# Attention and a two-matrix feed-forward on one core: the mean of the layer norm taken from the state's product by sums of float16 halves, paired high halves for the state's reads, and a new order of the work

## The chip, the cores and the metric

The kernel runs on one core of one Trainium2 chip. The metric is device time in microseconds (us) of one execution; lower is better. The kernel before took 707.6 us, the median of three runs (705.15 to 709.07).

The core has engines with queues of their own, each worked off in order: TensorE (PE in the profile, with its weight loads as PEld), VectorE (DVE), ScalarE (ACT), GpSimd (POOL), and SyncE (SP), which here only issues transfers. They meet through semaphores.

## What is computed

Cut to what matters, with B = 8 batches, H = 8 heads, S = 512 rows, Ns = 32 state rows per head and D = 64; the feed-forward's weights are 512x2048 and 2048x512:

```python
scores = scale * x @ state.T            # per batch and head, 512 x 32
xread  = softmax(scores) @ state        # 512 x 64 per head
scores2 = scale * state @ x.T           # 32 x 512
sread  = softmax(scores2) @ x           # 32 x 64 per head
x = concatenate([xread, sread])         # heads side by side: 544 rows of 512 per batch
mu, var = mean(x), mean((x - mu) ** 2)  # over the 512 columns
xn = (x - mu) / sqrt(var + 1e-06) * g_ln
out = x + maximum(xn @ w_ch1, 0) @ w_ch2
```

x and state come as float32, the weights as float64. Every large product is made of float16 halves: a high half and what is left of the number after it. A product of two such numbers is three matmuls (high by high, high by low, low by high), and with the halves laid side by side on the partitions sometimes fewer.

## The kernel before

**Row form.** The 512 rows of one batch never exist as normalized rows. Since xread is the softmax `ea` times the state, `xread @ w1` is `ea` times (`state @ w1`). So for each batch a `matrix` is made of the state and the first weight (`state_products`, lines 577 to 591: eight matmuls of 32x512 on four column groups at once, line 582, into one PSUM tile `acc`, for each of four units u of 512 hidden columns and two groups g of four heads). ScalarE takes its high half out of PSUM (line 590), VectorE the low half (line 591). `first_products` (line 605) multiplies `matrix` by `ea` (matmuls of line 616) into `acc`; `hidden` (line 595) takes each tile through a buffer `strip`, of which there are three: ScalarE writes the relu into `strip`, ScalarE the high half `hid`, and an engine subtracts for the low half. `second_products` (line 677) multiplies `hid` by the second weight (line 673), and VectorE adds the result to the residual `xr`.

**The mean.** Subtracting the row's mean is done on the weight before: `weights1(u)` (lines 498 to 538) loads float64 words (`raw`), makes float32 of them (`words`, `w_t`), gets the mean over the 512 rows of gain times weight by four float32 matmuls (`means`, line 516), and replaces `w_t` by gain times weight less that mean (line 519: four VectorE instructions on 128x512). Then ScalarE takes sizes (line 521), bfloat16 matmuls add them up (line 525), a scale comes of the largest sum, and the weight is split in a high and a low half (line 531, 128x2048 at once). Four transfers (line 538) lay the halves out as `w1c`: for each k of 128 rows, index s of 0 or 1 picks 64 rows, which stand on the partitions twice, as high half and as low half.

**The state's own rows.** The 8x32 rows `sread` of all batches go to DRAM, come back as two tiles of 128 rows, and are normalized and split in `state_hidden` (line 636). Their product with `w1c` (line 657) is 16 matmuls of 128x256 for each 128 hidden columns: eight with the high half of the rows standing twice, eight with the low half standing twice. 4 units, 4 times 128 columns each, make 256 matmuls.

**Order of the work.** Every step is yielded by a generator as one item; `issue` (line 190) takes items of several generators by strings such as "c3 c1 a0-1", a letter for the generator and numbers for its items. `PLAN` orders the prologue (weights, batch 0 with products taken by units, batch 1, attention of batch 2), `BATCH` one round for each of the batches 2 to 5 (products of batch b with the attention and the state products of b + 1), `LAST` the rest. So the order on each engine's queue is what these strings say. Transfers are nearly all on SP's queue.

**Names used below.** `s_j` is the state of a batch, laid out 32 rows of four heads on the partitions; `x_am` the largest size in it, from which its scale comes; `sh` its halves; `sT` these, transposed by a transfer. `banks` is the one PSUM tile of two banks that attention uses in turn: for scores (line 320), for the read of x by the softmax (line 396) and its fold (line 409), out of which VectorE takes `sread`, and for `mix` (line 432), which multiplies `ek` (a copy of `ea`, made by eight transfers and one more) by `sk` (halves of `s_r`, the state again). `mix` takes the tile over from `sread`.

Of the kernel before, what the change touches and what calls it, by code (L numbers as in the profile page):

```python
# [113 lines left out]
def moe_attention(ctx: ExitStack, tc: tile.TileContext, x, state, g_ln, w1, w2, out):  # L114

# [656 lines left out]
```

## Time and profile before

| what | us |
|---|---|
| median of three runs | 707.6 |
| profiled execution, its own time | 707.91 |
| its span in the trace | 706.1 |
| PE busy in the span | 655.7 |
| DVE busy | 370.9 |
| ACT busy | 365.3 |
| POOL busy | 68.0 |

The span is what the trace covers; the profiled execution took 1.8 us more than it. In the profile a group of instructions is named by line, engine, operation and output<-input; a line can be that of a helper (line 110 is the one that runs most items), so groups are told apart by their tiles. "Idle before" is the time that the engine stood still just before such instructions, with what released it. Matmuls are pipelined, so the mean of one matmul's record is longer than the step from one to the next; the chain of waits shows the step.

### The profile page before, as it was taken

How to read it: one execution, taken by the hardware profiler on the slowest of the kernel's cores; microseconds unless marked ns; L12 is line 12 of the kernel's file. 1: busy time of each engine (PE TensorE's matmuls, PEld its weight loads, DVE VectorE, ACT ScalarE, POOL GpSimd, SP SyncE). 2: the span in 40 equal slices, each digit the busy share in tenths (PEclk: the TensorE clock that was granted, in tenths of full speed). 3: DMA queues.
4: the chain of work that ended last, by engine and by line, in shares of the span. 5: the costliest groups of instructions: out<-in, count | busy, mean ns of one | idle time of the engine just before them, and what ended most of it. 6: DMA issues, size and time to landing. Idle time of an engine off the chain costs nothing.

```text
span 706.1 us, 10278 instructions
## 1 busy us (share of the span) xinstructions
PE 655.7 (93%) x4129; PEld 320.8 (45%) x4132; DVE 370.9 (53%) x670; ACT 365.3 (52%) x588; POOL 68.0 (10%) x54
## 2 busy tenths in 40 slices
PE   1565989999999999899999999999999999999997
PEld 0232645444453444444444444444444345445763
DVE  5995889655624454354635462545365834421120
ACT  5585889986413933295419541773287545410220
POOL 0000463211200002000200020002000200000000
PEclk9867899999999999999999999999999999999999
DMA  8988794636251032503070306130524060140001
GB/s 325 326 217 197 232 209 119 123 74 135 59 138 61 8 60 55 148 30 68 16 185 32 68 8 162 63 64 8 124 90 68 1 135 5 59 61 1 31 31 30
DMA packets 97392, 67.52 MB, mean 96 GB/s; under 512 B 73600, under 2 KB 89472, under 8 KB 96896
## 3 DMA queue, kind: packets, MB, share of 16 engines
q1 hardware_dynamic: 95424, 63.19, 35.1%
q0 software_dynamic: 864, 3.15, 2.5%
q8 instruction: 32, 0.52, 0.3%
q10 hardware_dynamic: 1056, 0.53, 0.3%
q14 instruction: 16, 0.13, 0.1%
HBM read 28.05 MB, written 9.44 MB: 53 GB/s over the span
## 4 chain that ended last, share of the span: by engine, by line
PE 70%; DVE 9%; DMA 8%; SPq 5%; ACT 4%; POOL 2%; issue 1%; POOLq 0%; DVEq 0%; ACTq 0%
PE acc L673 37%; PE acc L616 20%; SPq L110 5%; PE acc L657 4%; PE acc L582 3%; DMA w1c<-raw 2%; POOL ts L110 2%; DVE w_t L110 2%; PE acc L516 2%; DMA s_j<-in_state_dram 1%; DMA s_r<-in_state_dram 1%; PE banks L432 1%; DMA raw<-in_moe_w_ch_dram 1%; DVE raw L110 1%; DMA ebT<-eb 1%
## 5 line engine op out<-in xcount | busy, mean ns | idle before, releaser
L673 PE MATMUL acc<-w2h,hid 128*128 128x512 f16 x1632 | 368.2, 382 | 0.0
L673 PEld LDWEIGHTS <-hid 128*128 128x128 f16 x1632 | 158.2, 99 | 192.7 <-issue 12.6
L616 PE MATMUL acc<-ea,matrix 128*128 128x512 f16 (+1 forms) x864 | 176.1, 356 | 1.0 <-DVE matrix L110 0.7
L616 PEld LDWEIGHTS <-matrix 128*128 128x128 f16 x864 | 82.6, 98 | 84.6 <-issue 5.5
L110 DVE TENSOR_TENSOR hid<-strip,hid 128x512 f16<-128x512 f32 x120 | 81.2, 697 | 71.4 <-ACT hid L110 71.1
L110 ACT ACTIVATE strip<-acc,hs 128x512 f32<-128x512 f32 x112 | 75.5, 681 | 53.5 <-PE acc L616 29.6
L110 ACT ACTIVATE hid<-strip 128x512 f16<-128x512 f32 x136 | 83.0, 626 | 7.6 <-PE acc L673 4.9
L110 ACT ACTIVATE matrix<-acc 128x512 f16<-128x512 f32 x64 | 36.2, 602 | 64.1 <-PE acc L582 64.1
L110 DVE SCALAR_TENSOR_TENSOR xr<-acc,of_second,xr 128x512 f32<-128x512 f32 x28 | 21.0, 748 | 64.7 <-PE acc L673 64.6
L110 DVE SCALAR_TENSOR_TENSOR matrix<-acc,matrix 128x512 f16<-128x512 f32 x64 | 41.8, 680 | 20.8 <-ACT matrix L110 20.7
L582 PE MATMUL acc<-w1c,sT 128*32 128x512 f16 x512 | 38.2, 397 | 10.7 <-DMA w1c<-raw 10.3
L110 POOL TENSOR_TENSOR ts<-ts,mA 128x1024 f32<-128x1024 f32 (+1 forms) x8 | 16.1, 2016 | 232.8 <-DVE mA L110 202.6
L110 ACT ACTIVATE strip<-acc,hr 128x512 f32<-128x512 f32 x8 | 5.4, 686 | 49.4 <-PE acc L657 49.4
L110 POOL TENSOR_TENSOR rs<-rs,mhalf 128x4 f32<-128x4 f32 (+1 forms) x10 | 9.5, 955 | 199.6 <-DVE rs L110 199.6
L657 PE MATMUL acc<-xsT,w1c 128*128 128x256 f16 x256 | 28.4, 273 | 0.0
L110 POOL TENSOR_TENSOR hid<-strip,hid 128x512 f16<-128x512 f32 x16 | 22.1, 1405 | 58.7 <-ACT hid L110 58.6
L110 DVE SCALAR_TENSOR_TENSOR x<-x_f,x_s,x 128x512 f16<-128x512 f32 x32 | 25.3, 804 | 4.4 <-ACT x L110 4.3
L657 PEld LDWEIGHTS <-w1c 128*128 128x128 f16 x256 | 25.1, 98 | 3.5
L110 ACT ACTIVATE xr<-banks,ux 128x1024 f32<-128x1024 f32 x14 | 15.7, 1119 | 20.2 <-PE banks L432 20.2
L110 ACT ACTIVATE ea<-ef 128x1024 f16<-128x1024 f32 (+1 forms) x9 | 8.5, 958 | 33.5 <-DVE ef L110 33.5
L110 DVE BATCH_NORM_STATS2 s<-xr 128x6 f32<-128x512 f32 x32 | 21.4, 686 | 8.1 <-ACT xr L110 7.5
L582 PEld LDWEIGHTS <-sT 128*32 128x32 f16 x512 | 10.4, 97 | 30.5 <-issue 24.0
(112 smaller groups left out, 514.4 us busy)
## 6 DMA issues: line engine op xcount, KB each, us to landing
raw<-in_moe_w_ch_dram SPq DMA_DIRECT2D x16, 1024.0 KB, 8.2
out_dram<-xr SPq DMA_DIRECT2D x16, 512.0 KB, 2.7
x_f<-in_x_dram SPq DMA_DIRECT2D x15, 512.0 KB, 5.9
w1c<-raw SPq DMA_DIRECT2D x16, 256.0 KB, 6.9
ek<-ea SPq DMA_DIRECT2D x56, 64.0 KB, 2.1
ek<-ek SPq DMA_DIRECT2D x7, 512.0 KB, 4.4
xr<-part POOLq DMA_DIRECT2D x6, 512.0 KB, 5.3
s_r<-in_state_dram SPq DMA_DIRECT2D x28, 64.0 KB, 4.1
```

The lines of the kernel that those rows point to most:

```text
L110: return lambda: f(*map(now, args), **{k: now(v) for k, v in kw.items()})
L432: nc.tensor.matmul(px[:, c, D * h:D * h + D], lhsT=ek[:, h // 4, h % 4, (2 * t + c) * P:(2 * t + c + 1) * P], rhs=sk[:, h], start=True, st ...
L516: nc.tensor.matmul(ps, lhsT=gm[:, k:k + 1].broadcast_to([P, P]), rhs=t4[:, k], start=k == 0, stop=k == 3)
L582: nc.tensor.matmul(ps[32 * j:32 * j + 32], lhsT=sT[:, g, a, 32 * j:32 * j + 32], rhs=w[:, 2 * g + j // 2, j % 2], start=a == 0, stop=a == ...
L616: nc.tensor.matmul(o, lhsT=m[:, g, i, P * q:P * q + P], rhs=ea[:, s, k, g], start=g == 0 and n == 0 and (b > 0 or q % 2 == 0), stop=g == 1 ...
L657: nc.tensor.matmul(ps[:, 256 * f:256 * f + 256].rearrange("p (t n) -> p t n", t=2), lhsT=w[:, k // 2, k % 2, P * (q + f):P * (q + f) + P], ...
L673: nc.tensor.matmul(po, lhsT=hid[:, i, q, c * P:(c + 1) * P], rhs=w[:, j, q], start=first and q == 0 and n == 0, stop=last and q == 3 and n ...
```

## The change

**The mean** is no longer taken from the weight. The gain goes into the split: a column `gs` is gain times scale, and the split is done for each k by itself, in quarters of 128x512. Sizes are taken of the weight without gain, and the adding matmuls have the gain (`gb`) as their other side. Eight float16 matmuls (`add_up`) sum the split halves over all rows, and ScalarE keeps the result, `sums_of_inputs[:, u]`, in the buffer `convert`, which is thereby no longer free for raw words. For each batch VectorE makes `mean`, the mean of each state row (two small instructions). In `state_products` VectorE now first writes a `strip`: sums times mean, plus the tile in PSUM (the mean has a minus sign); both halves of `matrix` are taken of the strip.

**The state's rows.** Before their product, eight transfers (`high_halves`) put the high halves of two neighbouring 64-row pieces on one set of 128 partitions, in the buffers `extra_0` and `extra_1`. The low half of the rows is transposed once, not twice, and multiplied by these: four matmuls in place of eight, 12 in place of 16.

**Order.** All three strings are new. Two of the four last stores of each tile of the state's rows go to ScalarE's queue. Constants CM and SB change by a factor of two.

The core of the diff:

```diff
 PLAN = (
-    "b1 b3-4 b2 b0 b5 a0 b6-11 b22 b72 b12 d0 d3 b23-25 b13 b15 b14 b17-18 d2 d4 d1 d6 b19-20 d5 d7 e1 e5-6 e0 "
+    "d0 b0-1 b3 b2 b4-6 b16 b7-12 b17 c1 c0 d1 a0 d3 b24-25 b21-22 b13-14 b26-27 c6 b15 e1 c5 c7 e0 b18 c3 m2 "
...
     def gain():
-        yield do(nc.vector.tensor_scalar, gm, gx, 1.0 / DM, None, ALU.mult)
+        yield do(nc.scalar.activation, gb, gx.unsqueeze(2).broadcast_to([P, C, P]), AF.Abs, scale=1.0 / SW)
...
+        mean = Later(lambda: main.tile([P, G], F32, name=f"mean_{b % 2}"))
+        yield do(nc.vector.tensor_reduce, mean, sj, AX.X, ALU.add)
+        yield do(nc.vector.tensor_scalar, mean, mean, sst, -1.0 / DM, ALU.mult, ALU.mult)
...
         raws = ((wide(0, "raw"), wide(1, "raw")), (wide(2, "raw"), wide(3, "raw")), (extra(0, "raw"), extra(1, "raw")),
-                (odd("raw"), spare("raw")))[u]
+                (odd("raw"), wide(0, "raw")))[u]
...
-        def means(ps, t4):
-            for k in range(4):
-                nc.tensor.matmul(ps, lhsT=gm[:, k:k + 1].broadcast_to([P, P]), rhs=t4[:, k], start=k == 0, stop=k == 3)
-        yield do(means, ps, t4)
-        for k in range(4):
-            yield do(nc.vector.scalar_tensor_tensor, t4[:, k], t4[:, k], gx[:, k:k + 1], ps, ALU.mult, ALU.subtract)
...
+        yield do(nc.vector.tensor_scalar, gs, gx, scale, None, ALU.mult)
         hl = raws[1].bitcast(F16).rearrange("p (i e) -> p i e", i=2)
-        yield from split(hl[:, 0], hl[:, 1], t, scale)
+        for k in range(4):
+            yield from split(*(hl[:, i, 512 * k:512 * k + 512] for i in range(2)), t4[:, k], gs[:, k:k + 1])
...
+        def add_up(ps, hl):
+            for i in range(2):
+                for k in range(4):
+                    nc.tensor.matmul(ps, lhsT=ones, rhs=hl[:, i, k], start=i == 0 and k == 0, stop=i == 1 and k == 3)
+        yield do(add_up, ps, hl)
+        yield do(nc.scalar.activation, sums_of_inputs[:, u], ps, AF.Copy)
...
                 yield do(multiply, ps, g, sT, w1c[u])
-                yield do(nc.scalar.activation, m[:, g, 0], ps, AF.Copy, scale=CM)
-                yield do(nc.vector.scalar_tensor_tensor, m[:, g, 1], ps, CM, m[:, g, 0], ALU.mult, ALU.subtract)
+                strips[0] += 1
+                v = block(2, f"strip_{strips[0] % 3}", 1, "strip")
+                yield do(nc.vector.scalar_tensor_tensor, v, sums_of_inputs[:, u], mean[:, g:g + 1], ps, ALU.mult, ALU.add)
+                yield do(nc.scalar.activation, m[:, g, 0], v, AF.Copy, scale=CM)
+                yield do(nc.vector.scalar_tensor_tensor, m[:, g, 1], v, CM, m[:, g, 0], ALU.mult, ALU.subtract)
...
+    def high_halves():
+
+        for t in range(2):
+            pair = extra(t, "high").bitcast(F16).rearrange("p (u k f) -> p u k f", u=2, k=4)
+            for u in (2 * t, 2 * t + 1):
+                high[u] = pair[:, u % 2]
+                for s in range(2):
+                    half = slice(64 * s, 64 * s + 64)
+                    yield do(nc.sync.dma_start, out=high[u][half], in_=w1c[u][half, :, s])
...
-                for k in range(H):
-                    for a in range(2):
-                        nc.tensor.matmul(ps[:, 256 * f:256 * f + 256].rearrange("p (t n) -> p t n", t=2),
-                                         lhsT=w[:, k // 2, k % 2, P * (q + f):P * (q + f) + P], rhs=xsT[:, :, a, k],
-                                         start=f == 0 and k == 0 and a == 0, stop=k == H - 1 and a == 1,
-                                         skip_group_check=True)
+                fs = slice(P * (q + f), P * (q + f) + P)
+                for k in range(12):
+                    nc.tensor.matmul(ps[:, 256 * f:256 * f + 256].rearrange("p (t n) -> p t n", t=2),
+                                     lhsT=w[:, k // 2, k % 2, fs] if k < H else wn[:, k - H, fs], rhs=xsT[:, :, k],
+                                     start=f == 0 and k == 0, stop=k == 11, skip_group_check=True)
...
-            yield do(nc.sync.dma_start, out=out[4 * t + j, S:S + NS, :], in_=results[B][0][1][t][32 * j:32 * j + 32, 0])
+            yield do((nc.sync, nc.scalar)[j % 2].dma_start, out=out[4 * t + j, S:S + NS, :],
+                     in_=results[B][0][1][t][32 * j:32 * j + 32, 0])
```

**What the strings move, at three places.** The number behind a tile's name only tells one use of it from another.

First, VectorE's queue in a round of `BATCH`, around `sread`. Before:

```order
L110 TENSOR_SCALAR rB_3393<-rB_3393,x_i_3083 128x2
L110 TENSOR_REDUCE x_am_3670<-s_j_3668 128x1
L110 TENSOR_TENSOR sread_3502<-banks_3421,rB_3393 128x128
L110 SCALAR_TENSOR_TENSOR matrix_3500<-acc_3491,matrix_3500 128x512
L110 SCALAR_TENSOR_TENSOR xr_2839<-acc_3156,of_second_3389,xr_2839 128x512
L110 BN_STATS s6_3531<-xr_3529 128x6
```

And now:

```order
L113 SCALAR_TENSOR_TENSOR strip_3627<-sums_370,mean_0_3125,acc_3606 128x512
L113 SCALAR_TENSOR_TENSOR strip_3629<-sums_370,mean_0_3125,acc_3618 128x512
L113 SCALAR_TENSOR_TENSOR xr_2982<-acc_3477,of_second_3247,xr_2982 128x512
L113 TENSOR_SCALAR rB_3490<-rB_3490,x_i_3213 128x2
L113 TENSOR_TENSOR sread_3651<-banks_3573,rB_3490 128x128
L113 SCALAR_TENSOR_TENSOR matrix_3555<-strip_3629,matrix_3555 128x512
L113 SCALAR_TENSOR_TENSOR matrix_3653<-strip_3627,matrix_3653 128x512
```

Ahead of `sread` stood `x_am`, which reads the next batch's `s_j`. It has moved behind, into the next round, and two strips stand a little ahead of `sread` instead.

Second, SP's queue in the same round, from the state's transpose to the next batch's loads. Before:

```order
L110 DMA_TRANSPOSE sT_0_3153<-sh_92 128x4x128
L110 DMA_TRANSPOSE xT_3241<-x16_2986 128x16x128 x2
L110 DMA s_r_3645<-in_state_dram 32x8x64
L110 DMA ek_3385<-ea_3381 32x2x512 x2
L110 DMA_TRANSPOSE ebT_3419<-eb_3369 128x16x128
L110 DMA ek_3385<-ea_3381 32x2x512 x6
L110 DMA ek_3385<-ek_3385 64x4096
L110 DMA x_f_3647<-in_x_dram 128x4x256
L110 DMA s_r_3645<-in_state_dram 32x8x64
L110 DMA s_j_3668<-in_state_dram 128x2x64
```

And now:

```order
L113 DMA_TRANSPOSE sT_0_3223<-sh_92 128x4x128
L113 DMA s_r_3070<-in_state_dram 32x8x64
L113 DMA s_j_3777<-in_state_dram 128x2x64
L113 DMA_TRANSPOSE xT_3376<-x16_3132 128x16x128
L113 DMA s_r_3070<-in_state_dram 32x8x64
L113 DMA_TRANSPOSE xT_3376<-x16_3132 128x16x128
L113 DMA_TRANSPOSE ebT_3474<-eb_3471 128x16x128
L113 DMA s_r_3779<-in_state_dram 32x8x64
L113 DMA ek_3497<-ea_3495 32x2x512 x8
L113 DMA ek_3497<-ek_3497 64x4096
```

The next batch's `s_j` has moved from behind the copies of `ek` to a place right behind `sT`, ahead of both transposes of x, and the transpose `ebT` no longer stands between the copies.

Third, VectorE's queue in the prologue, at the first split of a weight (unit 0). Before:

```order
L110 SCALAR_TENSOR_TENSOR w1_t_181<-w1_t_181,gx_75,acc_296 128x512 x2
L110 SCALAR_TENSOR_TENSOR ea_290<-ef_288,ea_290 128x512
L110 SCALAR_TENSOR_TENSOR w1_t_181<-w1_t_181,gx_75,acc_296 128x512
L110 RECIPROCAL of_weights_217<-is1_262 128x1
L110 SCALAR_TENSOR_TENSOR eb_307<-eB_304,eb_307 128x1024
L110 SCALAR_TENSOR_TENSOR raw_142<-w1_t_140,of_weights_217,raw_142 128x2048
```

And now:

```order
L113 TENSOR_SCALAR gs_0_217<-gx_75,of_weights_205 128x4
L113 SCALAR_TENSOR_TENSOR w1_t_203<-raw_152 128x1024
L113 TENSOR_SCALAR is1_212<-of_weights_205 128x1
L113 SCALAR_TENSOR_TENSOR raw_129<-w1_t_150,gs_0_217,raw_129 128x512
L113 STREAM_TRANSPOSE ts_233<-banks_194 128x512
L113 RECIPROCAL of_weights_205<-is1_212 128x1
```

The low half of unit 0 stood as one piece behind the gain's instructions of unit 2 and part of batch 0's softmax; now its first quarter stands two instructions behind its column `gs`.

More of the change, by code (lines that the diff above doesn't have):

```diff
@@ L28 @@
 SW = 2.0**13
-CM = 2.0**-14
+CM = 2.0**-15
 SH = 2.0**-12
-SB = 2.0**14
+SB = 2.0**15
 SR = 2.0**-6
@@ L223, in moe_attention @@
     nc.vector.memset(mhalf, -0.5)
-    ones = main.tile([P, P], BF16, name="ones")
-    nc.vector.memset(ones, 1.0 / SW)
+    ones = main.tile([P, P], F16, name="ones")
+    nc.vector.memset(ones, 1.0)
     ids = main.tile([P, 2, 2], F32, name="ids")
@@ L248, in absmax @@
         return do(nc.vector.tensor_reduce, a, t, AX.X, ALU.max, apply_absolute_value=True)
-    gm = main.tile([P, C], F32, name="gm")
+    gb = main.tile([P, C, P], BF16, name="gb")
+    sums_of_inputs = block(8, "convert", 1, "sums").rearrange("p (u f) -> p u f", u=U)
     def gain():
-        yield do(nc.vector.tensor_scalar, gm, gx, 1.0 / DM, None, ALU.mult)
+        yield do(nc.scalar.activation, gb, gx.unsqueeze(2).broadcast_to([P, C, P]), AF.Abs, scale=1.0 / SW)
     sh = main.tile([P, G, 2, 2, D], F16, name="sh")
@@ L329, in attention @@
         ea = block(4, f"ea_{b % 2}", 1, "ea").bitcast(F16).rearrange("p (s i g t) -> p s i g t", s=parts, i=2, g=G)
-        results.append((residual(b, "xr"), sT, ea, Later(lambda: main.tile([P, C], F32, name=f"rf_{b % 2}"))))
+        results.append((residual(b, "xr"), sT, ea, Later(lambda: main.tile([P, C], F32, name=f"rf_{b % 2}")), mean))
         mA, dA = column("mA", 32), column("dA", 32)
@@ L506, in weights1 @@
         raws = ((wide(0, "raw"), wide(1, "raw")), (wide(2, "raw"), wide(3, "raw")), (extra(0, "raw"), extra(1, "raw")),
-                (odd("raw"), spare("raw")))[u]
+                (odd("raw"), wide(0, "raw")))[u]
         t = unit(u, "w1_t")
         scale, m = of_weights[:, u, 0:1], of_weights[:, u, 2:3]
+        gs = Later(lambda: main.tile([P, C], F32, name=f"gs_{u}"))
         yield from words(src, raws, t)
         t4 = t.rearrange("p (k f) -> p k f", k=4)
-        ps, total = accumulator(), accumulator()
-        def means(ps, t4):
-            for k in range(4):
-                nc.tensor.matmul(ps, lhsT=gm[:, k:k + 1].broadcast_to([P, P]), rhs=t4[:, k], start=k == 0, stop=k == 3)
-        yield do(means, ps, t4)
-        for k in range(4):
-            yield do(nc.vector.scalar_tensor_tensor, t4[:, k], t4[:, k], gx[:, k:k + 1], ps, ALU.mult, ALU.subtract)
         sizes = raws[0].bitcast(BF16)[:, 0:2048]
         yield do(nc.scalar.activation, sizes, t, AF.Abs)
+        total, ps = accumulator(), accumulator()
         def add(total, v):
             for k in range(4):
-                nc.tensor.matmul(total, lhsT=ones, rhs=v[:, 512 * k:512 * k + 512], start=k == 0, stop=k == 3)
+                nc.tensor.matmul(total, lhsT=gb[:, k], rhs=v[:, 512 * k:512 * k + 512], start=k == 0, stop=k == 3)
         yield do(add, total, sizes)
@@ L546, in weights2 @@
         raws = ((wide(2, "raw"), wide(3, "raw")), (extra(0, "raw"), extra(1, "raw")), (odd("raw"), wide(3, "raw")),
-                (extra(1, "raw"), spare("raw")))[u]
-        t = (wide(1, "w2_t"), spare("w2_t"), extra(0, "w2_t"), odd("w2_t"))[u]
+                (extra(1, "raw"), wide(3, "raw")))[u]
+        t = (wide(1, "w2_t"), wide(2, "w2_t"), extra(0, "w2_t"), odd("w2_t"))[u]
         s, am, m, top, inv = (of_weights[:, U + u, k:k + 1] for k in range(5))
@@ L575, in moe_attention @@
     matrix = [[None] * U for _ in range(B)]
+    strips = [0]
     def state_products(b):
@@ L583, in multiply @@
                                      rhs=w[:, 2 * g + j // 2, j % 2], start=a == 0, stop=a == 1, skip_group_check=True)
-        sT = results[b][1]
+        sT, mean = results[b][1], results[b][4]
         for u in range(U):
@@ L589, in state_products @@
                 yield do(multiply, ps, g, sT, w1c[u])
-                yield do(nc.scalar.activation, m[:, g, 0], ps, AF.Copy, scale=CM)
-                yield do(nc.vector.scalar_tensor_tensor, m[:, g, 1], ps, CM, m[:, g, 0], ALU.mult, ALU.subtract)
-    strips = [0]
+                strips[0] += 1
[3 more added lines that the diff above has]
+                yield do(nc.vector.scalar_tensor_tensor, m[:, g, 1], v, CM, m[:, g, 0], ALU.mult, ALU.subtract)
     def hidden(ps, scale, hi, lo, n, engine=nc.vector):
@@ L634, in first_products @@
                                           nc.gpsimd)
+    high = [None] * U
+    def high_halves():
[6 more added lines that the diff above has]
+                    yield do(nc.sync.dma_start, out=high[u][half], in_=w1c[u][half, :, s])
     def state_hidden():
         xr = results[B][0][1]
-        xsT = rows("xsT").bitcast(F16).rearrange("p (t a h n) -> p t a h n", t=2, a=2, h=H)
+        xsT = rows("xsT").bitcast(F16)[:, 0:24 * P].rearrange("p (t k n) -> p t k n", t=2, k=12)
         mv, rs = yield from moments([xr[t][:, 0] for t in range(2)])
@@ L643, in state_hidden, with multiply @@
             yield do(nc.vector.tensor_scalar, xn, xr[t][:, 0], mv[:, t, 0:1], rs[:, t:t + 1], ALU.subtract, ALU.mult)
-            v = xn.rearrange("p (h d) -> p h d", h=H).unsqueeze(2).broadcast_to([P, H, 2, D])
-            pc = halves("pc").rearrange("p (a h i d) -> p a h i d", a=2, h=H, i=2)
-            yield do(nc.scalar.activation, pc[:, 0], v, AF.Copy, scale=SN)
-            for i in range(2):
-                yield do(nc.vector.scalar_tensor_tensor, pc[:, 1, :, i], xn.rearrange("p (h d) -> p h d", h=H), SN,
-                         pc[:, 0, :, i], ALU.mult, ALU.subtract)
-            yield do(nc.sync.dma_start_transpose, out=xsT[:, t].rearrange("p a h n -> p (a h) n"),
-                     in_=pc.rearrange("p a h i d -> p (a h i d)"))
-        def multiply(ps, q, w, xsT):
-            for f in range(2):
-                for k in range(H):
-                    for a in range(2):
-                        nc.tensor.matmul(ps[:, 256 * f:256 * f + 256].rearrange("p (t n) -> p t n", t=2),
-                                         lhsT=w[:, k // 2, k % 2, P * (q + f):P * (q + f) + P], rhs=xsT[:, :, a, k],
-                                         start=f == 0 and k == 0 and a == 0, stop=k == H - 1 and a == 1,
-                                         skip_group_check=True)
+            v = xn.rearrange("p (h d) -> p h d", h=H)
+            pc = halves("pc")[:, 0:12 * P]
+            hi = pc[:, 0:8 * P].rearrange("p (h i d) -> p h i d", h=H, i=2)
+            lo = pc[:, 8 * P:12 * P].rearrange("p (h d) -> p h d", h=H)
+            yield do(nc.scalar.activation, hi, v.unsqueeze(2).broadcast_to([P, H, 2, D]), AF.Copy, scale=SN)
+            yield do(nc.vector.scalar_tensor_tensor, lo, v, SN, hi[:, :, 0], ALU.mult, ALU.subtract)
+            yield do(nc.sync.dma_start_transpose, out=xsT[:, t], in_=pc)
+        def multiply(ps, q, w, wn, xsT):
+            for f in range(2):
+                fs = slice(P * (q + f), P * (q + f) + P)
[3 more added lines that the diff above has]
+                                     start=f == 0 and k == 0, stop=k == 11, skip_group_check=True)
         for u in range(U):
@@ L665, in state_hidden @@
                 ps = accumulator()
-                yield do(multiply, ps, q, w1c[u], xsT)
+                yield do(multiply, ps, q, w1c[u], high[u], xsT)
                 yield from hidden(ps, hr[:, u:u + 1], h[:, 0, q:q + 2, 0:256], h[:, 1, q:q + 2, 0:256], 2)
```

6 lines of the change are left out of this document (3 added, 3 removed), and 89 rows, old and new, of tables (BATCH, LAST, PLAN).

## The prediction

> **What bounds the kernel now.** I read the shares and slices of the page first, then busy time by stretches, then the chain of waits, then the queues of single engines where that chain leaves TensorE. The page's busy times and three rows of its slices:
>
> ```profile
> PE 655.7 (93%) x4129; PEld 320.8 (45%) x4132; DVE 370.9 (53%) x670; ACT 365.3 (52%) x588; POOL 68.0 (10%) x54
> ...
> PE   1565989999999999899999999999999999999997
> ...
> DVE  5995889655624454354635462545365834421120
> ...
> PEclk9867899999999999999999999999999999999999
> ```
>
> Busy time by stretch (window, length, busy time with instructions on PE, PEld, DVE, ACT, POOL, then granted clock, DMA share, GB/s):
>
> ```profile
> 10.50:99.40 88.90, 58.99 (x465) 33.93 (x469) 75.56 (x123) 64.00 (x89) 15.30 (x11) 0.85 0.94 251
> 0.00:102.20 102.20, 62.69 (x495) 36.48 (x499) 81.37 (x140) 69.23 (x100) 18.80 (x19) 0.87 0.92 255
> 102.20:300.00 197.80, 194.28 (x1199) 90.45 (x1198) 108.91 (x205) 111.97 (x180) 27.16 (x22) 0.99 0.38 90
> 300.00:706.10 406.10, 398.70 (x2440) 193.83 (x2436) 180.58 (x327) 184.06 (x311) 22.02 (x14) 0.99 0.25 58
> ```
>
> There are two kernels here. Up to about 102 us PE stands idle 39.5 us (102.20 less 62.69), with VectorE busy 75.56 of 88.90 us and the transfers at a share of 0.94. Behind it PE is the bound: idle 3.5 us, then 7.4 us. So PE work taken out behind 102 us counts in full, VectorE work there (busy about half) counts only where PE waits for it, and in the prologue it is the other way round.
>
> Where PE still waits in the steady part, its rows show three places, one in each of three rounds (start, length, what, idle before and releaser):
>
> ```profile
> 293.32 0.77 PE L432 MATMUL banks<-sk,ek 128*128 128x64 f16 x16 [1.95 <-DMA s_r<-in_state_dram]
> 366.85 0.77 PE L432 MATMUL banks<-sk,ek 128*128 128x64 f16 x16 [0.63 <-DVE sread L110]
> 439.75 0.77 PE L432 MATMUL banks<-sk,ek 128*128 128x64 f16 x16 [1.69 <-DMA s_r<-in_state_dram]
> ```
>
> The releaser named twice is a transfer of s_r, the one in the middle is sread. VectorE's queue and SP's issues at the first of the three tell which:
>
> ```profile
> 292.70 0.29 DVE L110 TENSOR_REDUCE x_am<-s_j 128x1 f32<-128x128 f32 x1 [4.38 <-DMA s_j<-in_state_dram]
> 292.97 0.29 DVE L110 TENSOR_TENSOR sread<-banks,rB 128x128 f32<-128x128 f32 x1
> ```
>
> ```profile
> 284.48 0.51 SPq L110 DMA_DIRECT2D ek<-ek  x1
> ...
> 287.72 0.47 SPq L110 DMA_DIRECT2D s_j<-in_state_dram  x1
> ```
>
> VectorE stood 4.38 us waiting for the next batch's s_j, issued only at 287.72; sread, queued behind, ended at 293.26, and mix started at 293.32. So mix waits for its PSUM tile, which sread still reads, and all three gaps have this cause by their timing. The chain shows what follows two of them:
>
> ```profile
> 256.24 2.59 PE acc L673 x12
> ...
> 294.08 4.28 PE acc L673 x12
> ...
> 367.62 2.59 PE acc L673 x12
> ...
> 440.52 4.28 PE acc L673 x12
> ...
> 651.04 13.97 PE acc L657 x128
> ```
>
> Twelve matmuls of L673 take 2.59 us (0.216 each), behind the gaps of 1.95 and 1.69 us they take 4.28, 1.69 more each; behind 0.63 us they don't. The three gaps and two slow groups come to 1.95 + 0.63 + 1.69 + 2 x 1.69 = 7.65 us.
>
> **The change, part by part.** The sum is made against the profiled execution (707.9 us: span 706.1 and 1.8 outside), which lies 0.3 above the median.
>
> *The state's rows.* Of 256 matmuls of L657 64 go. By the chain's row one takes 13.97 / 128 = 0.109 us, and PE is the bound there: **-7.0**. The eight transfers that pair the halves are queued with the last batch; one 128x512 subtraction per tile instead of two goes too, hidden before the transposes.
>
> *Stores.* The end of the trace:
>
> ```profile
> 699.62 4.32 SPq L110 DMA_DIRECT2D out_dram<-xs  x8
> 701.44 0.75 DVE L110 SCALAR_TENSOR_TENSOR xs<-acc,of_second,xs 128x512 f32<-128x512 f32 x1 [1.84 <-PE acc L673]
> ```
>
> Eight issues take 4.32 us, 0.54 each, four of them behind the last addition (ends 702.19). With two on another queue, two issues go from the end: **-1.0** (0 to -1.1).
>
> *Steady waits.* s_j is now loaded right behind sT, a batch ahead, and x_am has left its place before sread. So 7.65 goes. What is late next at mix is the copy of ek:
>
> ```profile
> ek<-ek SPq DMA_DIRECT2D x7, 512.0 KB, 4.4
> ```
>
> Issued at 284.48 it landed about 288.9; PE came to mix at 291.37 (293.32 less 1.95). It is covered by some 2.5 us, and in the new strings, where PE work and softmax between scores and mix are of like length, I put the margin at 2. I count **-7.65**.
>
> The Trainium skill ("TensorE: Matmul & The Clock Gate", section "What's actually happening") has the clock halved only after an idle window of about 3.4 us in a free-running raster. By that, gaps of 1.95 and 1.69 us could not be what slows the matmuls. The slow groups agree with its half speed (1.69 lost is 3.4 us at half rate), the short gaps ahead of them disagree with its threshold.
>
> *The mean, steady part.* Each batch gets eight strips on VectorE and two small sums. Nearest rows:
>
> ```profile
> L110 DVE SCALAR_TENSOR_TENSOR xr<-acc,of_second,xr 128x512 f32<-128x512 f32 x28 | 21.0, 748 | 64.7 <-PE acc L673 64.6
> L110 DVE SCALAR_TENSOR_TENSOR matrix<-acc,matrix 128x512 f16<-128x512 f32 x64 | 41.8, 680 | 20.8 <-ACT matrix L110 20.7
> L110 ACT ACTIVATE matrix<-acc 128x512 f16<-128x512 f32 x64 | 36.2, 602 | 64.1 <-PE acc L582 64.1
> L110 DVE BATCH_NORM_STATS2 s<-xr 128x6 f32<-128x512 f32 x32 | 21.4, 686 | 8.1 <-ACT xr L110 7.5
> L616 PE MATMUL acc<-ea,matrix 128*128 128x512 f16 x672 | 154.1, 379 | 0.9 <-DVE matrix L110 0.7 <-ACT matrix L110 0.2
> ```
>
> A strip has the operands of xr<-acc: 0.748 us, 64 in all 47.9 us, 6 us per batch of some 73. VectorE's half-idle time hides them. They also lengthen the way from L582 to L616: 0.75 + 0.60 + 0.68 = 2.03 us instead of 1.28. Before, PE waited for matrix 0.9 us in all 672 matmuls. The last two products' matrices are the critical ones; other L616 groups of six (1.29 us in the chain, 6 x 0.216) stand between, three of them 3.9 us, so some 1.8 us remain for queueing on VectorE. If that cover went, 0.75 or more per boundary would show. For small new waits here and at mix I allow **+1.0** (0 to 3).
>
> *The prologue.* The rows of what goes and what is like the new:
>
> ```profile
> L516 PE MATMUL acc<-w_t,gm 128*128 128x512 f32 x32 | 18.8, 747 | 5.4 <-DVE w_t L110 5.4
> L110 DVE SCALAR_TENSOR_TENSOR w_t<-w_t,gx,acc 128x512 f32<-128x512 f32 x16 | 11.3, 738 | 0.7 <-PE acc L516 0.6
> L110 DVE SCALAR_TENSOR_TENSOR raw<-w_t,of_weights,raw 128x2048 f16<-128x2048 f32 x4 | 9.4, 2343 | 2.2 <-ACT raw L110 2.2
> L110 DVE SCALAR_TENSOR_TENSOR pc<-xn,pc 128x512 f16<-128x512 f32 x4 | 2.6, 688 | 2.2 <-ACT pc L110 2.2
> ```
>
> On VectorE 11.3 us go (the gain's 16). In come eight strips of batch 0 (6.0), sixteen quarters for four wholes (16 x 0.688 - 9.4 = 1.6; 0 if they cost by size), four gs and four small sums of batches 0 and 1, bounded by 0 and the 0.29 of x_am each, of which I take 1.7 in all, near the upper end: net -2.0. On PE 18.8 us of float32 go and 32 additions at 0.216 come (6.9), where PE isn't the bound. What else is gained is order: VectorE doesn't wait for PE's float32 sums, and the split starts earlier. Its waits there:
>
> ```profile
> 57.14 2.35 DVE L110 SCALAR_TENSOR_TENSOR raw<-w_t,of_weights,raw 128x2048 f16<-128x2048 f32 x1 [2.20 <-ACT raw L110]
> ...
> 69.94 1.23 DVE L110 SCALAR_TENSOR_TENSOR w_t<-raw 128x1024 uint32<-128x1024 uint32 x1 [3.81 <-DMA w1c<-raw]
> ...
> 73.71 0.69 DVE L110 TENSOR_REDUCE of_weights<-acc 128x1 f32<-128x512 f32 x1 [2.55 <-PE acc L525]
> ```
>
> Together 8.6 of 13.3 us idle (88.90 less 75.56). I take half of the 13.3, 6.6, as won, since quarters and an earlier split shorten the first and last of these waits, and nothing makes the transfers faster. PE's first second product comes so much earlier than now:
>
> ```profile
> 102.19 2.75 PE L673 MATMUL acc<-w2h,hid 128*128 128x512 f16 x12
> ```
>
> 102.2 - 6.6 - 2 = 93.6. But by the orders three groups of L582 of batch 1 (eight matmuls, about 0.6 us each) and one group of 12 L616 (1.3) now stand behind that point and not ahead, 3.1 us of PE work, and I allow 1 us of waits in the ramp that is earlier: -8.6 + 3.1 + 1 = **-4.5**. Bounds: all the idle time won, -15.3 + 4.1 = -11.2; nothing won, 0.
>
> Sum: -7.0 - 1.0 - 7.65 + 1.0 - 4.5 = -19.15, so 707.9 - 19.1 = **688.8 us**.
>
> **Rivals.**
> (A) *Transfers bound the prologue.* For it: their share of 0.94, and VectorE's longest wait of the three (3.81) is for one. Against: the share is lower, 0.92, over the whole prologue, and VectorE was waited for too. Prologue term 0: 693.3 us.
> (B) *The copy of ek takes sread's place at mix.* The margin of 2 us goes if its issue stands behind a transpose on SP's queue. Price: the gaps come back, 7.65 less the allowance already counted of 1.0: 695.4 us.
> (C) *Slower: the matrix comes late.* If VectorE is over 1.8 us late at the boundary of a batch (two BN_STATS of 0.686 and one strip queued ahead are enough), L616 waits, and a gap of 1.95 with its slow group costs 1.95 + 1.69 = 3.64. Eight batches have seven boundaries: 7 x 3.64 = 25.5. It decides from six of them on (21.8), against 20.15 won without the allowance: 707.9 - 20.15 + 25.5 = 713.3 us. Against: only 0.9 us of such waits before.
> (D) *Slow groups that are not due to the gaps.* Then only the idle 4.27 goes and 3.38 stays: 692.2 us. By the rule of the Trainium skill cited above this would be so.
> (E) *It doesn't do what it says* would mean the products are counted as before; the orders show 192 for 256 and no L516, so no chance goes to it.
>
> **How the numbers follow.** The forecast has 0.60, A 0.17, B 0.11, D 0.05, C 0.04, and 0.03 a mix of A, B and another stall that ends near no change. Low end: the prologue's best bound, stores at -1.1, no new waits, 707.9 - 7.0 - 1.1 - 7.65 - 11.2 = 681, and 2 for the spread of the runs shown: **679**. High end: A and B together, 693.3 + 6.65 = **700**. A measurement of this kernel tells about 0.5%, 3.5 us, from no change. All but C and the mix are faster by more: 0.93; the mix 0.03 within; C 0.04 slower.
>
> **What would show it.** Right: no idle time before mix, 2.59 us for every chain group of 12; the L657 group at 0.75 of its time; the first second product near 94 us; PE idle in the steady part under 5 us. Wrong: a first second product at 100 or later (A); idle before mix with ek landing last (B); idle before L616 released by matrix (C); slow groups of 12 with no gap ahead (D); strips far from 0.75 us.

## The result and the profile after

The changed kernel took 695.83 us (median of four runs, 693.92 to 698.0), the kernel before 706.38 beside it: ratio 0.9847, interval 0.9801 to 0.9892. A second set of runs, beside other experiments, gave 695.11 us and a ratio of 0.9832 (0.9807 to 0.9857). So 10.5 to 12.2 us were won where 19 were forecast. The profiled execution took 696.65 us (span 694.8), 11.3 us less than the one of before; the account below is made between these two.

The page's busy times and three of its slices rows, after:

```profile
PE 638.3 (92%) x4068; PEld 311.0 (45%) x4068; DVE 421.7 (61%) x747; ACT 375.1 (54%) x605; POOL 75.2 (11%) x54
...
PE   0536969999999999999999999999999999999997
...
DVE  5977899977734556665567557664766674521020
...
PEclk9976989999999999999999999999999999999999
```

Busy time by stretch, columns as before:

```profile
10.50:99.40 88.90, 50.89 (x459) 30.70 (x460) 75.74 (x130) 72.09 (x108) 16.86 (x11) 0.86 0.94 248
0.00:99.80 99.80, 51.81 (x462) 31.28 (x463) 79.56 (x144) 76.85 (x118) 17.55 (x17) 0.87 0.92 250
99.80:300.00 200.20, 196.29 (x1223) 91.80 (x1223) 134.04 (x237) 112.08 (x179) 32.85 (x23) 0.99 0.39 92
300.00:694.80 394.80, 390.18 (x2385) 187.94 (x2383) 208.15 (x368) 186.14 (x309) 24.82 (x14) 1.00 0.28 66
```

The first row is the one to set beside the row of before: VectorE is busy 75.74 of the same 88.90 us, where it was 75.56. Nothing of its 13.3 us of idle time was won. Behind 300 us PE now stands idle 4.6 us, nearly all of it behind the last matmul. All of PE's waits from 94 to 690 us, with the matmuls that they hold up:

```profile
100.17 4.71 PE L697 MATMUL acc<-w2h,hid 128*128 128x512 f16 x11 [5.31 <-DVE w2h L113]
109.59 0.38 PE L113 MATMUL spread<-ids,of_weights 1*128 1x1 f32 x2 [0.70 <-DVE of_weights L113]
133.43 0.27 PE L113 MATMUL spread<-idf,of_weights 128*1 128x128 f32 x1 [0.85 <-ACT raw L113]
208.69 0.94 PE L440 MATMUL banks<-sk,ek 128*128 128x64 f16 x16 [1.93 <-DMA sread_rows<-sread]
525.86 0.27 PE L113 MATMUL spread<-idf,x_am 128*2 128x128 f32 x1 [0.59 <-DVE x_am L113]
```

The three waits of `mix` in the rounds of `BATCH` are gone. What is new stands at the prologue's end: the first second product did one matmul at 94.48 and then stood 5.31 us for the other half of its weight, and its other eleven matmuls took 4.71 us, not 2.4. And `mix` has a wait of 1.93 us in a place where it had none, at batch 2. Lines of the chain of waits, for the rounds and the state's rows (now line 682):

```profile
302.40 13.06 PE acc L630 x60
...
373.20 13.06 PE acc L630 x60
...
444.01 13.06 PE acc L630 x60
...
628.37 7.86 PE acc L682 x72
```

A round takes 70.8 us, each like the next, and a matmul of L682 takes 7.86 / 72 = 0.109 us, as before.

### The profile page after: what moved, and what is told of

It is laid out like the page before. It is cut to its first block, busy times and chain, and to the rows that moved or that the text cites. A ratio compares the mean times of both kernels' runs of the same rounds, so it can differ in the third digit from the quotient of the medians.

```text
span 694.8 us, 10286 instructions
## 1 busy us (share of the span) xinstructions
PE 638.3 (92%) x4068; PEld 311.0 (45%) x4068; DVE 421.7 (61%) x747; ACT 375.1 (54%) x605; POOL 75.2 (11%) x54
## 4 chain that ended last, share of the span: by engine, by line
PE 81%; DVE 7%; DMA 5%; ACT 3%; SPq 2%; issue 1%; DVEq 0%; ACTq 0%
PE acc L697 50%; PE acc L630 20%; PE acc L595 4%; PE acc L682 3%; DMA w1c<-raw 3%; DMA raw<-in_moe_w_ch_dram 2%; SPq L113 2%; DVE w_t L113 2%; ACT raw L113 2%; DVE raw L113 1%; PE banks L440 1%; PE banks L404 1%; PE banks L417 1%; PE banks L328 1%; PE spread L113 1%
## 5 line engine op out<-in xcount | busy, mean ns | idle before, releaser
L630 PE MATMUL acc<-ea,matrix 128*128 128x512 f16 (+1 forms) x864 | 172.7, 356 | 0.0
L113 ACT ACTIVATE hid<-strip 128x512 f16<-128x512 f32 x136 | 83.7, 627 | 13.5 <-PE acc L697 10.5
L113 ACT ACTIVATE matrix<-strip 128x512 f16<-128x512 f32 x64 | 39.4, 626 | 85.6 <-DVE strip L113 85.4
L113 DVE SCALAR_TENSOR_TENSOR strip<-sums,mean,acc 128x512 f32<-128x512 f32 x64 | 46.4, 741 | 34.9 <-PE acc L595 34.0
L113 DVE SCALAR_TENSOR_TENSOR matrix<-strip,matrix 128x512 f16<-128x512 f32 x64 | 42.5, 683 | 9.7 <-ACT matrix L113 9.3
L113 POOL TENSOR_TENSOR rs<-rs,mhalf 128x4 f32<-128x4 f32 (+1 forms) x10 | 11.6, 1158 | 188.8 <-DVE rs L113 188.7
L113 POOL TENSOR_TENSOR hid<-strip,hid 128x512 f16<-128x512 f32 x16 | 24.9, 1595 | 29.3 <-ACT hid L113 29.3
L113 DVE SCALAR_TENSOR_TENSOR w_t<-raw 128x1024 uint32<-128x1024 uint32 x16 | 26.6, 1691 | 0.7 <-ACT raw L113 0.4
L113 DVE SCALAR_TENSOR_TENSOR x<-x_f,x_s,x 128x512 f16<-128x512 f32 x32 | 23.0, 744 | 0.5 <-ACT x L113 0.5
L113 ACT ACTIVATE x<-x_f,x_s 128x512 f16<-128x512 f32 x32 | 21.7, 711 | 2.3 <-DVE x_s L113 2.3
L113 ACT ACTIVATE raw<-raw 128x1024 f32<-128x1024 f32 x16 | 18.2, 1148 | 8.1 <-DMA raw<-in_moe_w_ch_dram 6.9
```

The lines of the kernel that those rows point to most:

```text
L113: return lambda: f(*map(now, args), **{k: now(v) for k, v in kw.items()})
L630: nc.tensor.matmul(o, lhsT=m[:, g, i, P * q:P * q + P], rhs=ea[:, s, k, g], start=g == 0 and n == 0 and (b > 0 or q % 2 == 0), stop=g == 1 ...
```

## The experiments

Every ratio is to the kernel before, run beside it on the same chip. Where a kernel is set against the changed kernel by ratios, the changed kernel counts as 0.984, the middle of its two results.

**One item of the kernel before moved.** `c11` is x_am. The section on the kernel says that the strings give each queue's order; this place shows the limit of that. `c11` is written early in a round, behind the whole round before, and yet the built queue has it ahead of that round's sread: in the built queue an item can stand ahead of items that were written before it.

```diff
-    "c3 c1 a0-1 c6 a8 a2 c2 c11 a9-10 c9 ... a12-13 c12-14 "
+    "c3 c1 a0-1 c6 a8 a2 c2 a9-10 c9 ... a12-13 c11 c12-14 "
```

> The kernel before with one item moved: the largest size of the next batch's s_j (x_am) is written behind the four sizes of x instead of ahead, which takes it out of sread's way on VectorE in all four rounds of BATCH; s_j is still loaded late. Theory: the three gaps before mix (1.95, 0.63, 1.69 us) and the two slow groups behind two of them go, 7.65 us, ratio to the kernel before 0.989. Rival D: the slow groups stay, only the 4.27 us of idle time go, ratio 0.994. Rival B: the copy of ek ends next and takes the place of sread, gaps of about the same size remain, ratio 0.997 to 1.

Measured: 700.09 us, ratio 0.9908 (0.9888 to 0.9928), 6.5 us won (5.1 to 7.9). The interval holds 7.65 and excludes rival B and rival D's 4.27. The chain in that run:

```profile
297.74 10.47 PE acc L616 x48
...
363.22 2.59 PE acc L673 x12
368.77 10.46 PE acc L616 x48
...
434.24 2.59 PE acc L673 x12
439.79 10.46 PE acc L616 x48
```

Rounds of 71.02 us, and 2.59 for the group of 12 that stands behind `mix`, where two of three were 4.28. s_j still came late (issued at 287.98, before at 287.72); only the instruction that waits for it stood elsewhere, and sread started at 288.67, before at 292.97:

```profile
287.98 0.47 SPq L110 DMA_DIRECT2D s_j<-in_state_dram  x1
```

So the transfer named as releaser was not the cause, the place of x_am was, and the slow groups went with the gaps.

**The new mean alone, under the old strings** (old numbers mapped to the new items, the rest as before).

```diff
-                yield do(nc.scalar.activation, m[:, g, 0], ps, AF.Copy, scale=CM)
-                yield do(nc.vector.scalar_tensor_tensor, m[:, g, 1], ps, CM, m[:, g, 0], ALU.mult, ALU.subtract)
+                v = ps
+                yield do(nc.vector.scalar_tensor_tensor, v, sums_of_inputs[:, u], mean[:, g:g + 1], ps, ALU.mult, ALU.add)
+                yield do(nc.scalar.activation, m[:, g, 0], v, AF.Copy, scale=CM)
+                yield do(nc.vector.scalar_tensor_tensor, m[:, g, 1], v, CM, m[:, g, 0], ALU.mult, ALU.subtract)
```

> The kernel before with the new mean alone, at the old orders: gain's float32 sums and 16 VectorE instructions out, quarters, sums of halves and strips in, placed where the old items stood. The strips are written in place in PSUM, and the second words of unit 3 are loaded behind the sums of unit 0, since their buffer now holds sums. The state's rows, the stores and the place of x_am are as before. Theory now: in the prologue VectorE loses as much as it gains and behind it the strips are hidden: no change within 3 us, ratio 0.996 to 1.004, and the gaps before mix stay. Rival, the prediction's term: the mean brings 4.5 us in the prologue, ratio 0.993. Rival C: strips make the matrices late at boundaries, idle time before L616-like products of 0.75 us or more each, ratio 1.01 or more.

Measured: 760.01 us, ratio 1.076 (1.072 to 1.0799): 53 us slower, and my theory was far off. PE's rows at three places:

```profile
61.31 1.87 PE L548 MATMUL acc<-raw,ones 128*128 128x512 f16 x4 [8.15 <-ACT sums L114]
...
131.10 2.75 PE L687 MATMUL acc<-w2h,hid 128*128 128x512 f16 x12 [0.67 <-DVE matrix L114]
...
263.83 12.56 PE L630 MATMUL acc<-ea,matrix 128*128 128x512 f16 x45 [6.45 <-ACT matrix L114]
```

Two causes can be seen. The eight additions of halves (L548), placed behind the transfers of their unit, stand in PE's queue and wait 8.15 us until ScalarE has taken other sums out of PSUM, and all that is behind them waits too (ScalarE's sums stand behind words for which it waited 11.31 us itself, for a transfer of raw words): the first second product comes at 131 us, not 102. And matrices come late behind the batches (6.45 us at the first), which is rival C's mechanism. The strings and the mean can't be priced apart: this run is one poor order of many, with strips in PSUM. It shows how much the places in the queues can decide.

**Unit 0's second half of w2h split right behind the first.**

```diff
-    ... h32 i18-19 j4 h24 h19 h28 j7 ... k6 i16-17 h23 ...
+    ... h32 i18 i16 i19 i17 j4 h24 h19 h28 j7 ... k6 h23 ...
```

> The changed kernel with one pair of items moved in the prologue: the second half of unit 0's second weight (w2h) is split right behind the first, ahead of two words (w_t) and a shift on VectorE. Theory: PE's first second product no longer stands 5.31 us, and the matmuls behind it are not slow (2.3 us): up to 7.6 us off, some of it taken by the next wait, 3 to 6 in all, ratio to the changed kernel 0.992 to 0.996 (to the kernel before about 0.978). Rival: transfers or unit 1's words bound the prologue, the wait comes back a few us later, ratio to the changed kernel 0.999 to 1.003.

Measured: 695.59 us, ratio 0.9845 (0.9822 to 0.9869): no change. The first second product now ran through, from 94.40, but two other waits came or grew:

```profile
99.46 2.29 PE L630 MATMUL acc<-ea,matrix 128*128 128x256 f16 x12 [2.32 <-ACT strip L113]
108.89 0.38 PE L113 MATMUL spread<-ids,of_weights 1*128 1x1 f32 x2 [3.58 <-DVE of_weights L113]
```

So the wait of 5.31 us was only where the lag showed. As I read it, PE waits for one thing or the other until VectorE has got through the words that stand in its queue; the run after the next bears that out.

**GpSimd's subtractions replaced by copies on ScalarE,** which leaves the subtraction out.

```diff
-        yield do(engine.tensor_tensor, lo, r, hi, ALU.subtract)
+        if engine is nc.gpsimd:
+            yield do(nc.scalar.activation, lo, r, AF.Copy)
+        else:
+            yield do(engine.tensor_tensor, lo, r, hi, ALU.subtract)
```

> The changed kernel, with the 16 subtractions of batch 0's hidden low halves that GpSimd does replaced by 16 copies on ScalarE, so the subtraction is left out. Theory: VectorE's word instructions (w_t) are slow (mean 1.69 us, where 1.22 without company) because GpSimd's subtractions run beside them; their mean falls to about 1.25, VectorE gains 6 to 7 us in the prologue, and the time falls by 2 to 5 us. Rival 1: the width of the operands or the transfers slow them: the mean stays over 1.6. Rival 2: they become fast, but the time doesn't fall, since ScalarE, now with 10 us more, or the transfers bound the prologue.

Measured: 693.79 us, ratio 0.9812 (0.9791 to 0.9834), 2 us less than the changed kernel, with intervals that overlap. The group of word instructions, in the changed kernel

```profile
L113 DVE SCALAR_TENSOR_TENSOR w_t<-raw 128x1024 uint32<-128x1024 uint32 x16 | 26.6, 1691 | 0.7 <-ACT raw L113 0.4
```

and in this run:

```profile
L113 DVE SCALAR_TENSOR_TENSOR w_t<-raw 128x1024 uint32<-128x1024 uint32 x16 | 19.1, 1221 | 1.1 <-ACT raw L113 1.1
```

1.69 against 1.22 us: the company of GpSimd's subtractions costs VectorE 7.5 us on these 16 instructions. Words and the shifts before them together took 39.4 us in this trace of the changed kernel, 38.8 in that of its second set (1.51 us a word, but slower shifts), and 30.1 without the company. What it costs the kernel is not settled by 2 us within the noise.

**Words without their low bits** (the three lowest bits of each weight are left out), and the changed kernel once more beside it.

```diff
-            yield do(nc.vector.tensor_scalar, low, low, 29, None, ALU.logical_shift_right)
-            yield do(nc.vector.scalar_tensor_tensor, t[:, 1024 * fh:1024 * fh + 1024].bitcast(U32), high.bitcast(U32),
-                     3, low, ALU.logical_shift_left, ALU.bitwise_or)
+            yield do(nc.vector.tensor_scalar, t[:, 1024 * fh:1024 * fh + 1024].bitcast(U32), high.bitcast(U32), 3, None,
+                     ALU.logical_shift_left)
```

> The changed kernel itself, beside the kernel before and the next three, so that differences of 2 us can be told: ratio to the kernel before 0.985, within 0.003, and a first second product that stands some 5 us for its weights.

> The changed kernel, with the weights' words made from the high half of each float64 alone: the 16 shifts of low words on VectorE (12.8 us) are left out and the 16 instructions that join two words become one-operand shifts (0.7 for 1.69 us, 15 us less). This leaves out the three lowest bits of each weight. Transfers are the same. Theory (VectorE, and with it its company on GpSimd, holds up the prologue): the time falls by 4 to 10 us against the changed kernel, ScalarE comes next. Rival A (transfers bound the prologue): under 1.5 us.

Measured: 686.05 us, ratio 0.9698 (0.9678 to 0.9718), 9.1 us less than the 695.11 of the changed kernel beside it. The stretches of this run:

```profile
10.50:99.40 88.90, 56.96 (x492) 34.13 (x493) 65.31 (x125) 74.86 (x115) 16.88 (x12) 0.94 0.97 266
```

VectorE is busy 65.3 us, where it was 75.7, and the transfers move 266 GB/s, where they moved 248: in the new order VectorE's work on the words holds up the prologue, and transfers don't. This is also the fastest version here, at the price of those bits.

**The same edit in the kernel before.**

> The kernel before, with words from the high half of each float64 alone: 16 shifts (0.75 us each, 11.9 us) out and the joining instructions at 0.7 for 1.22 us (8 us less). Theory: VectorE bounded the prologue of the kernel before too, 4 to 9 us faster. Rival: there the transfers of w1c bound it (PE waited 6.6 us for one), under 1.5 us.

Measured: 705.06 us, ratio 0.998 (0.9959 to 1.0): 1.4 us won, by the interval at most 2.9. So VectorE hardly bound the kernel before there. PE's waits are those of before:

```profile
68.79 0.59 PE L582 MATMUL acc<-w1c,sT 128*32 128x512 f16 x1 [6.90 <-DMA w1c<-raw]
...
89.80 0.38 PE L582 MATMUL acc<-w1c,sT 128*32 128x512 f16 x1 [2.96 <-DMA w1c<-raw]
```

**GpSimd's subtractions on VectorE**, in the changed kernel and in the one without low bits.

```diff
                         yield from hidden(ps, scale, *(h[:, i, q:q + 2, 256 * s:256 * s + 256] for i in range(2)), 2,
-                                          nc.gpsimd)
+                                          nc.vector)
```

> The changed kernel, with the 16 subtractions of batch 0's hidden low halves on VectorE in place of GpSimd; nothing is left out. VectorE gets 16 x 0.69 = 11 us more and loses what company costs it (7.5 us on its word instructions, about 2 elsewhere). Theory: about even, 2 us faster to 2 us slower than the changed kernel, with words at 1.22 us again. Rival (it is VectorE's sum of work alone that counts, company costs nothing): 5 us or more slower.

> The changed kernel with words from the high half of each float64 alone, as in the run that took the shifts out, and besides the 16 subtractions of batch 0's low halves on VectorE in place of GpSimd. Theory: VectorE now has idle time for the 11 us, and no company slows it: 0 to 3 us faster than without the second edit, 683 to 686 us. Rival: VectorE is still the bound, 2 us or more slower, as this edit was with the shifts in (3.4 us).

Measured: 698.49 us (0.9869, 0.9848 to 0.989), 3.4 us slower; and 695.71 us (0.9831, 0.9809 to 0.9854), 9.4 us slower by the ratios than the same without it. My theory expected neither. The second is in the range of the rival, but not for its reason: VectorE was not the bound by its work (60.5 us busy of 88.9). The words of the first came down to 1.33 us only, not to 1.22. PE's row and three rows of VectorE and ScalarE in the second:

```profile
94.61 2.72 PE L630 MATMUL acc<-ea,matrix 128*128 128x256 f16 x12 [2.80 <-ACT strip L113]
```

```profile
91.36 1.28 DVE L113 SCALAR_TENSOR_TENSOR w2h<-w_t,of_weights,w2h 128x1024 f16<-128x1024 f32 x1 [2.71 <-ACT w2h L113]
...
93.16 0.69 DVE L113 TENSOR_TENSOR hid<-strip,hid 128x512 f16<-128x512 f32 x1
```

```profile
93.96 0.60 ACT L113 ACTIVATE strip<-acc 128x512 f32<-128x512 f32 x1 [2.64 <-DVE hid L113]
```

PE waits for ScalarE's strips, and ScalarE for a strip buffer. There are three, each free only when its subtraction is done. Here the subtraction (93.16) stood in VectorE's queue behind a split of w2h that waited 2.71 us for ScalarE, and ScalarE's next strip waited 2.64 us for the subtraction. In the changed kernel GpSimd's queue held nothing but these subtractions up to 103 us. So a queue of their own was worth more here than what its company costs VectorE.

**Strips twice**, for batches 2 to 7.

```diff
-                yield do(nc.vector.scalar_tensor_tensor, v, sums_of_inputs[:, u], mean[:, g:g + 1], ps, ALU.mult, ALU.add)
+                one = do(nc.vector.scalar_tensor_tensor, v, sums_of_inputs[:, u], mean[:, g:g + 1], ps, ALU.mult, ALU.add)
+                yield one if b < 2 else (lambda f: lambda: (f(), f()))(one)
```

> The changed kernel, with every strip of batches 2 to 7 computed twice: 48 more VectorE instructions of 0.74 us, 36 us in all, on the path from a state product to its matrix. Theory (PE bounds there and the strips are hidden): within 1.5 us of the changed kernel, PE's waits behind 300 us below 2 us more than in it. Rival C: the matrices are late at the batches' boundaries, 0.75 us or more at each of six, 4.5 us or more.

Measured: 699.45 us, ratio 0.9887 (0.9866 to 0.9909), 4.3 us slower, between the two. In each round a new wait of 0.35 us stands, one of them quoted, and behind the rounds others came or grew, the one quoted last from 0.59 to 1.83:

```profile
338.90 5.35 PE L698 MATMUL acc<-w2h,hid 128*128 128x512 f16 x24 [0.35 <-DVE strip L113]
...
528.69 0.27 PE L113 MATMUL spread<-idf,x_am 128*2 128x128 f32 x1 [1.83 <-DVE x_am L113]
```

36 us more of VectorE's work cost 4.3: seven eighths are hidden, and in the rounds the cover is used up by a strip's second computation.

**Matmuls of the state's rows 16 again, and the last stores on one queue**, two kernels.

```diff
-                for k in range(12):
+                for n, k in enumerate((*range(12), *range(8, 12))):
```

```diff
-            yield do((nc.sync, nc.scalar)[j % 2].dma_start, out=out[4 * t + j, S:S + NS, :],
+            yield do(nc.sync.dma_start, out=out[4 * t + j, S:S + NS, :],
```

> The changed kernel with 16 matmuls per 128 hidden columns of the state's rows again, the four with the paired high halves done twice (so the low half of the rows counts twice), 64 matmuls more at 0.109 us. Theory (PE bounds there): 7.0 us slower than the changed kernel, ratio to the kernel before 0.993. Rival (something else ends last there, such as the reading out of PSUM): 3 us or less.

> The changed kernel with all eight last stores on one queue. Theory: two issues of 0.54 us each come back at the end, by the traces 0.65 to 1.1 us slower than the changed kernel, at the edge of what can be told; in the trace the span ends 3.9 us behind the last matmul, not 3.2. Rival: nothing, since both queues feed the same DMA engines.

Measured: 702.01 us (0.9928, 0.9907 to 0.995), 6.2 us slower by the ratios, near 64 x 0.109 = 7.0; and 696.52 us (0.9839, 0.9816 to 0.9863), which can't be told from no change. The end of the trace with one queue, the issues of each of the two tiles by themselves:

```profile
688.58 1.76 SPq L113 DMA_DIRECT2D out_dram<-xs  x4
...
690.39 0.75 DVE L113 SCALAR_TENSOR_TENSOR xs<-acc,of_second,xs 128x512 f32<-128x512 f32 x1 [1.84 <-PE acc L697]
...
691.17 1.73 SPq L113 DMA_DIRECT2D out_dram<-xs  x4
```

and of the changed kernel, the issues of the last tile:

```profile
690.80 0.75 DVE L113 SCALAR_TENSOR_TENSOR xs<-acc,of_second,xs 128x512 f32<-128x512 f32 x1 [1.84 <-PE acc L697]
...
691.58 0.78 SPq L113 DMA_DIRECT2D out_dram<-xs  x2
...
691.59 0.85 ACTq L113 DMA_DIRECT2D out_dram<-xs  x2
```

From VectorE's end to the span's: 695.1 - 691.14 = 3.96 us with one queue, 694.8 - 691.55 = 3.25 with two. The two win 0.7 us, not 1.1. An issue takes 0.43 us on one queue (1.73 / 4) and no more on two (0.85 / 2), so two fewer behind the last addition are 0.87 us; the stores then land after up to 2.0 us, where they took 1.7 on one queue. The row of 4.32 us for eight issues holds the wait between the two tiles, so 4.32 / 8 = 0.54 is not the time of an issue.

## Why the prediction was right in direction and too large

The time lies in the range (679 to 700), 7 us above the forecast of 688.8. Step by step:

- *The state's rows, -7.0.* Right: 0.109 us per matmul after too, and 6.2 us by the run that puts the 64 back.
- *Stores, -1.0.* 0.7 by the traces. The term was made of two issues of 0.54 us, and an issue takes 0.43; besides, the last stores land a little later.
- *Steady waits, -7.65.* Right in cause and size: 6.5 (5.1 to 7.9) from moving x_am alone. The releaser that the profile named was wrong twice, the timing on VectorE's queue was right. Rival D fell with this. B happened in small, once: the 1.93 us at batch 2's `mix`. The releaser named there is again a transfer that `mix` does not need. The last copy of ek, issued at 199.94, took 8.6 us to land, not 4.4, so it came at 208.5, just ahead of `mix` at 208.69; the trace of the second set names it:

```profile
199.94 0.53 SPq L113 DMA_DIRECT2D ek<-ek  x1
...
ek<-ek SPq DMA_DIRECT2D x1, 512.0 KB, 8.6
```

```profile
210.07 0.94 PE L440 MATMUL banks<-sk,ek 128*128 128x64 f16 x16 [1.45 <-DMA ek<-ek]
```

- *New waits, +1.0.* 1.9 at that place. A strip takes 0.74 us, as forecast, and the strips are hidden as they are, but the doubled ones show that little cover is left, so rival C had a real mechanism at a small price. Under the old strings it was large.
- *The prologue, -4.5.* This is the step that failed, at "I take half of the 13.3, 6.6, as won" and at "net -2.0". The start alone came as forecast: the first second product's first matmul ran at 94.48, where 93.6 was expected. But it needs both halves of its weight, w2h, and VectorE was done with them at 100.11 (97.94 + 2.17), where before it was done at 99.38 (96.47 + 2.91). VectorE's rows before:

```profile
96.47 2.91 DVE L110 SCALAR_TENSOR_TENSOR w2h<-w_t,of_weights,w2h 128x1024 f16<-128x1024 f32 x2
```

and after:

```profile
92.18 4.28 DVE L113 SCALAR_TENSOR_TENSOR w_t<-raw 128x1024 uint32<-128x1024 uint32 x2
...
97.94 2.17 DVE L113 SCALAR_TENSOR_TENSOR w2h<-w_t,of_weights,w2h 128x1024 f16<-128x1024 f32 x1
```

So nothing was won on VectorE up to there. Its busy time in the stretch is 75.74 for 75.56, though the new work had about the size that was forecast (strips 5.8 us, quarters 1.9 more than the wholes, gs 0.9). The 2 us saved were taken back by instructions that moved into the stretch (sk's low half, 1.75 us) and by slower ones: its twelve words took 16.2 us for 14.5, and the rest of the 7.5 us that GpSimd's company costs the words lies behind the stretch. The words of the stretch before:

```profile
L110 DVE SCALAR_TENSOR_TENSOR w_t<-raw 128x1024 uint32<-128x1024 uint32 x12 | 14.5, 1218 | 5.0 <-DMA w1c<-raw 4.9
```

and after:

```profile
L113 DVE SCALAR_TENSOR_TENSOR w_t<-raw 128x1024 uint32<-128x1024 uint32 x12 | 16.2, 1379 | 0.5 <-ACT raw L113 0.4
```

VectorE's idle time is 13.2 for 13.3: the waits for w1c's transfers (4.9 us) went and the one for the whole-width split shrank (2.2 to 0.8), but the waits for PE's sums (2.5 to 4.1) and ScalarE's matrices (2.4 to 3.8) grew and one for ScalarE's `ea` came (2.4). Counted from 99.8 (100.17 less the one matmul done), the first second product was 2.4 us earlier than before. What now stands behind that point takes more than that: the moved groups, three of L582 at 0.49 (the chain has 16 matmuls at 0.98) and one of L616 at 1.3, 2.8 us; and the slow eleven matmuls 2.3 (4.71 less 11 x 0.216). So the term is -2.4 + 2.8 + 2.3 = +2.7, a miss of 7.2.

Together: -7.0 - 0.7 - 7.65 + 1.9 + 2.7 = -10.75, where 11.3 was measured between the two profiles. PE's other waits behind the prologue come to 2.1 us, where they were 1.8, so about 0.9 us are not accounted for.

Rival A had the outcome (nothing won in the prologue) and half of the reason. By the runs without low bits VectorE hardly bound the kernel before there, but it does bound the changed one, by 9 us. That the transfers bound the one before, as A said, fits PE's waits for w1c there; no run made them lighter, so it is not shown. The earlier start of the split bought nothing that PE could use. What stays open is how much of the prologue's time GpSimd's company costs: 7.5 us on VectorE's words is shown, 2 us of time is within the noise.

## What to carry to other kernels

Idle time of the busiest engine in a stage is not there to be won by halves: look for what each wait would be replaced by, and price the new order by its own queues, since the new mean under the old strings cost 53 us. Where a wait is put down to a transfer, look at the queue of the engine that releases the tile: an instruction that waits for something else may stand ahead of the one that is needed, and moving that one instruction alone won 6.5 us here. And a wait that is removed in a stage whose engine is full comes back elsewhere: leave out some of that engine's work once, to see which engine bounds the stage, before moving items.
